# Attention, top-1 experts and a gated product on one core: when expert results leave, where two preparations stand, and which engine makes 24 low halves

## The chip, the cores and the metric

One core of a Trainium2 chip runs the whole program. The metric is the device time of one execution in microseconds (us); of the kernel before there are three runs, 886.69 to 887.77 us, median 887.34. A profiled execution is a run of its own, with its own time and span.

The engines that the text names: PE (TensorE, matrix products), ACT (ScalarE), DVE (VectorE), POOL (GpSimd) and SP (SyncE, which here only issues transfers). Each works its own list of instructions in order and waits on semaphores for the others.

## The reference

Three parts follow one another on 2304 tokens of width 512:

- attention: 4 batches x 8 heads, 576 positions of width 64, causal with a window of 128 and a slope per head; `scores = q k^T / 8 - slope * distance`, softmax over the window, times v. The heads of a token side by side are its 512 numbers x.
- top-1 experts: `e = argmax(x @ w_gate)` over 8 experts, `out = gate * sigmoid(x @ w_output_gate)[e] * (relu(x @ w1[e]) @ w2[e])`, hidden width 1024; gate is the softmax value of e.
- gated product: `g = x @ w_gate`, `out = (g * sigmoid(g) * (x @ w_val)) @ w_out`, hidden width 1536.

All is float32. The inputs are q, k and v, the experts' weights and the gated product's weights.

## The kernel before

A float32 operand is held as two halves, a high part that ACT makes by a copy into the type fp32r and a low part, the rest, that DVE or POOL makes by a subtraction. Each product is three passes (high x high, high x low, low x high), so a high and a low half of every weight and every activation have to be there in time.

**Attention and routing** (to about 160 us) go block by block over 128 tokens. For each group of blocks the routing counts the tokens of each expert and gives each token a row: DVE's `ohb` (L597, the one-hot choice), `gs` (L599, counts), `expf` (L601), `base` (L603), then PE counts those ahead, then DVE's `rk` (L616), `rankf` (L620), `sli` (L622). By `sli` the weighted tokens are scattered into the DRAM buffer `xs`, sorted by expert. At the end `expert_tables` sorts the experts by their counts, so that the experts p = 0 to 7 run from the fullest to the emptiest, with caps of 384, 384, 352, 336, 304, 272, 256 and 256 rows.

**Experts.** For p = 0 to 7 there are two products. The first makes `oh` in 8 steps m of 12 matmuls (L1089); ACT makes `hh` = relu(oh) (L1097) and DVE `hl`, the low half (L1100). The second makes the four results `oy` in 8 steps kk of 12 matmuls (L1114) from `hh` and `hl`; in its first four steps PE transposes the next expert's tokens (`tx`, L1016), which ACT and DVE split. A result leaves by `store_y`: ACT copies `oy` from PSUM to a buffer `y` (L1051) and issues its transfer to the DRAM buffer `ys` (L1053). The pool `sp` has two buffers under the tag "sc", which y shares with `sg` and `av` of the last part. At the end of an expert `store_y(2)` lets two results go, and the other two go one by one behind the next expert's steps m = 0 and m = 1; behind the last expert all four go at its end.

**Gated product** (from 414.95 us in the profile). Six units of 384 tokens, each of 12 steps (`wide_step`): `gate` and `val` (12 matmuls each, L1198); ACT's sigmoid `sg` (L1209), DVE's `sg` times gate (L1210) and `av` (L1211), ACT's `hh` (L1212), DVE's `hl` (L1213). Three steps later PE adds the step's share of the result `oo` (L1156). Tokens come by `load_unit` from `ys` (`xr<-ys`, L1026) and are split at L1034 and L1035.

**Weights** stream behind all this. SP loads them into one of LA = 7 staging buffers (`raw` of the experts, L340; `rawd` of the gated product, which are stored as 64-bit numbers, L345). A list `plan` gives each step of the experts and of the first wide unit the weights that it prepares, by `behind_step`, which calls `w_item` for each: for an expert's weight ACT's copy (L373) and a subtraction (L375) by DVE or, for each third, POOL. A half of a weight of the gated product takes `narrow`: ACT's L313 and L315, DVE's L321 and L324, and, one item later (`behind_half`), ACT's copy (L365) and the subtraction L366 on the engine that `behind_step` passes: POOL for p up to 6, DVE from the last expert on.

**Order.** From the end of attention a manual schedule holds: each engine's list is in the order in which the code is written, SP's too. Before that line a scheduler orders by dependencies. In it, before the first expert's tokens, stand `load_x(0)`, `expert_tables()`, a sigmoid of one number (L1070), 48 matmuls that keep PE busy (`keep_warm`), and `late_low`, which makes the low halves of the first expert's weights (L390) whose high halves were copied at L389.

Of the kernel before, what the change touches and what calls it, by code (L numbers as in the profile page):

```python
# [28 lines left out]
def attn_moe_glu_kernel(ctx, tc, q, k, v, w_gate, w_ogate, w1, w2, w2_gate, w2_val, w2_out, out, caps=CAPS):  # L29
    nc = tc.nc  # L30
# [63 lines left out]
    with ExitStack():  # L94
# [231 lines left out]
            )  # L326
            return lo.bitcast(F32)

        loaded = []
        sorted_known = [False]  # L330

        def w_load():
            while wjobs and len(loaded) < LA:
                name, kk, c, src = wjobs[-1]
                if name[1] > 0 and not sorted_known[0]:
                    return
                wjobs.pop()
                if c is None:
                    t = stg.tile([128, 512], F32, tag="stg", name="raw")
                    r = nc.sync.dma_start(out=t, in_=src())  # L340
                    if not sorted_known[0]:
                        tc.add_manual_dep(r.ins, pace[0].ins.name, DATA, reason="after the loads of the first rows")
                else:
                    t = stg.tile([128, 256, 2], I32, tag="stg", name="rawd")
                    nc.sync.dma_start(out=t.rearrange("p f b -> p (f b)"), in_=src())  # L345
                loaded.append((name, kk, c, t))

        w_late = []

        halves, n_rows = [], [0]  # L350

        def slot_of(name, kk, c):
            if kk % 2 == 0 and not c:
# [439 lines left out]


        wB[0] = wctx.enter_context(tc.tile_pool(name="wB", reuse_waits="tile", bufs=NBS))
        ht_p = wctx.enter_context(tc.tile_pool(name="ht", reuse_waits="tile", bufs=1))
        xe_p = wctx.enter_context(tc.tile_pool(name="xe", reuse_waits="tile", bufs=1))
        xr_p = wctx.enter_context(tc.tile_pool(name="xr", reuse_waits="tile", bufs=1))
        s_p = wctx.enter_context(tc.tile_pool(name="sp", reuse_waits="tile", bufs=2))
        tb_p = wctx.enter_context(tc.tile_pool(name="tb", reuse_waits="tile", bufs=1))  # L800
        ps_m = wctx.enter_context(tc.tile_pool(name="ps_m", reuse_waits="tile", bufs=8, space=PSUM))
# [5 lines left out]
        def tb(name, shape, dt=F32):  # L807
            return tb_p.tile([128] + shape, dt, tag=name, name=name)
# [3 lines left out]
        def scratch():  # L812
# [5 lines left out]
        TT, TS, STT, RED = (  # L818
            nc.vector.tensor_tensor, nc.vector.tensor_scalar, nc.vector.scalar_tensor_tensor, nc.vector.tensor_reduce)

        def expert_tables():

            cnt_ps = ps_m.tile([128, E], F32, tag="m", name="cnt_ps")
            for i in range(NGR):
                nc.tensor.matmul(out=cnt_ps, lhsT=ones, rhs=gs[:, i, :], start=(i == 0), stop=(i == NGR - 1))
            nc.vector.tensor_copy(cnt[:, 0, :], cnt_ps)
            key, srt = tb("key", [E]), tb("srt", [E])
            STT(out=key, in0=cnt[:, 0, :], scalar=float(E), in1=ktab, op0=ALU.mult, op1=ALU.add)
            nc.vector.max(out=srt, in_=key)
            ki, ci = tb("ki", [E], I32), tb("ci", [E], I32)  # L830
            nc.vector.tensor_copy(ki, srt)
            TS(out=reg[:, 0, :], in0=ki, scalar1=E - 1, scalar2=E - 1, op0=ALU.bitwise_and, op1=ALU.bitwise_xor)
            for p in range(1, E):
                e_reg[p] = nc.sync.value_load(reg[0:1, 0, p:p + 1], min_val=0, max_val=E - 1)
            TS(out=ci, in0=ki, scalar1=(1 << 15) - 1, scalar2=3, op0=ALU.bitwise_and, op1=ALU.logical_shift_right)
            held, end, off, ep = (tb(nm, [1, E]) for nm in ("held", "end", "off", "ep"))
            nc.vector.tensor_copy(ep[:, 0, :], reg[:, 0, :])
            nc.vector.tensor_copy(held[:, 0, :], ci)
            TT(out=held, in0=held, in1=capt, op=ALU.min)
            nc.vector.tensor_copy(end[:, :, 0:1], held[:, :, 0:1])  # L840
            for p in range(1, E):
                TT(out=end[:, :, p:p + 1], in0=end[:, :, p - 1:p], in1=held[:, :, p:p + 1], op=ALU.add)
            nc.vector.tensor_copy(total, end[:, :, E - 1:E])
            TT(out=off, in0=end, in1=held, op=ALU.subtract)
            nc.vector.tensor_copy(reg[:, 1, :], off[:, 0, :])

            own, pick = (t[:, 0:E, :] for t in scratch())
            TT(out=own, in0=iota8.unsqueeze(2).to_broadcast([128, E, E]), in1=ep.to_broadcast([128, E, E]),
               op=ALU.is_equal)
            for src, dst in ((off, offe), (capt, cape)):  # L850
                TT(out=pick, in0=own, in1=src.to_broadcast([128, E, E]), op=ALU.mult)
                RED(out=dst.rearrange("p a e -> p e a"), in_=pick, axis=AX, op=ALU.add)
# [123 lines left out]
            nc.vector.tensor_copy(er[:, 1, :], first[0:1, :, 0])  # L976
            nc.scalar.dma_start(out=ov_er[:, :, :], in_=er)

        xr, xe = {}, {}


        def raw_tile():
# [21 lines left out]
        def emit_xT(p, kks=range(KD)):  # L1004
            if p >= E:
                return
            n = caps[p]
            cb = -(-n // 128)
            r = xr[p]
            if p not in xe:  # L1010
                xe[p] = [grid(t, KD, n) for t in pair_tile(xe_p, "x", KD * cap)]
            xh, xl = xe[p]
            for kk in kks:
                t = ps_m.tile([128, CP], F32, tag="m", name="tx")
                for c in range(cb):
                    nc.tensor.transpose(t[:, c * 128:c * 128 + 128], r[:, c, kk * 128:kk * 128 + 128], ident)  # L1016
                nc.scalar.activation(out=xh[:, kk, :], in_=t[:, 0:n], func=AF.Copy)
                TT(out=xl[:, kk, :], in0=t[:, 0:n], in1=xh[:, kk, :], op=ALU.subtract)
# [38 lines left out]
        def behind_step():  # L1057
            st = step_no[0]
            step_no[0] += 1
            p = st // STEPS  # L1060
            for w in plan[st]:
                assert loaded[0][0:3] == w[0:3]
                w_item(nc.gpsimd if p < E - 1 else nc.vector)
            if p < E:
                next(tokens, None)

        with tc.manual_schedule(engines=ALL_ORDERED):
            load_x(0)
            expert_tables()
            nc.scalar.activation(out=tb("sig", [1]), in_=ident[:, 0:1], func=AF.Sigmoid)  # L1070
            sorted_known[0] = True
            keep_warm(ps_m, "m", 48)
            late_low(3)
            emit_xT(0)
            load_x(1)
# [4 lines left out]
            for p in range(E):  # L1080
# [3 lines left out]
                for m in range(KF):  # L1084
                    o = ps_m.tile([128, cap], F32, tag="m", name="oh")
                    i = 0
                    for a, b in PASSES:
                        for kk in range(KD):
                            nc.tensor.matmul(  # L1089
                                out=o[:, 0:n],  # L1090
                                lhsT=wt["w1", p, m // 4, kk][:, a, (m % 4) * 128:(m % 4) * 128 + 128],
                                rhs=(xh, xl)[b][:, kk, :],
                                start=(i == 0),
                                stop=(i == 3 * KD - 1),
                            )
                            i += 1
                    nc.scalar.activation(out=hh[:, m, :], in_=o[:, 0:n], func=AF.Relu)  # L1097
                    if p == 0 and m > 0:
                        off_reg[m] = nc.scalar.value_load(reg[0:1, 1, m:m + 1], min_val=0, max_val=NT)
                    STT(out=hl[:, m, :], in0=o[:, 0:n], scalar=0.0, in1=hh[:, m, :], op0=ALU.max, op1=ALU.subtract)  # L1100
                    if m % 4 == 3:
                        freed[0] += 2
                    store_y(1)
                    behind_step()
                    if p == E - 1 and m == 4:
                        load_unit(0)
                if p == E - 1:
                    wide_x = [[grid(t, KD, WU) for t in pair_tile(xe_p, "x", KD * cap)]]
                    x2[0] = wide_x[0]
                o = [ps_m.tile([128, cap], F32, tag="m", name="oy") for _ in range(KD)]  # L1110
                for kk in range(KF):
                    for d in range(KD):
# [17 lines left out]
                            load_x(p + 2)  # L1130
                    behind_step()
                y_left.extend((p, d, o[d][:, 0:n], n) for d in range(KD))
                store_y(2 if p < E - 1 else KD)
            load_unit(1)
            for _ in tokens:
                pass

# [77 lines left out]
        with tc.manual_schedule(engines=ALL_ORDERED):  # L1215
            for u in range(NW):
                for m in range(KF2):
                    s = u * KF2 + m
                    wide_step(u, m)
                    if u == 0:  # L1220
                        behind_step()
                        if not loaded:
                            behind_half(nc.vector)
                    if 7 <= m < 7 + KD and u + 1 < NW:
                        if m == 7:
                            x2[u + 1] = wide_x[(u + 1) % 2]
                        split_part(u + 1, m - 7)
# [134 lines left out]
```

## Time and profile before

| | |
|---|---|
| median of 3 runs | 887.34 us (886.69 to 887.77) |
| profiled execution, its own time | 891.87 us |
| its span | 890.2 us |
| mean granted clock | 0.978 of 2.4 GHz |
| PE busy | 845.7 us (95%) |
| DVE busy | 463.9 us (52%) |
| ACT busy | 396.1 us (44%) |
| POOL busy | 193.9 us (22%) |
| chain that ended last | PE 60%, DVE 13%, ACT 11%, transfers 7% |

The span is the profiled execution from its first to its last instruction; 1.7 us of its own time lie around it. In the rows further down, a time at the start of a row is in us from the span's start, the next number is how long the instruction took, and what stands in brackets is how long the engine was idle before and what ended that. "x4" joins four instructions of the same kind. ACTq and SPq are issues of transfers by ACT and SP. PEclk is the granted clock of PE as a share of 2.4 GHz.

### The profile page before, as it was taken

How to read it: one execution, taken by the hardware profiler on the slowest of the kernel's cores; microseconds unless marked ns; L12 is line 12 of the kernel's file. 1: busy time of each engine (PE TensorE's matmuls, PEld its weight loads, DVE VectorE, ACT ScalarE, POOL GpSimd, SP SyncE). 2: the span in 40 equal slices, each digit the busy share in tenths (PEclk: the TensorE clock that was granted, in tenths of full speed). 3: DMA queues.
4: the chain of work that ended last, by engine and by line, in shares of the span. 5: the costliest groups of instructions: out<-in, count | busy, mean ns of one | idle time of the engine just before them, and what ended most of it. 6: DMA issues, size and time to landing. Idle time of an engine off the chain costs nothing.

```text
span 890.2 us, 15339 instructions
## 1 busy us (share of the span) xinstructions
PE 845.7 (95%) x5463; PEld 776.5 (87%) x5463; DVE 463.9 (52%) x1268; ACT 396.1 (44%) x1063; POOL 193.9 (22%) x293
## 2 busy tenths in 40 slices
PE   7999989799999998899897999999999999999995
PEld 4777766699999998898897999999999999999994
DVE  6678886685575576567688523322322322232231
ACT  6898982163355576566666421121211212122110
POOL 3668875031122343330000010010001001001001
PEclk9999999899999999989998999999999999999998
DMA  9999522547547767665443020010002002000001
GB/s 230 261 282 243 140 73 84 178 131 218 176 143 223 249 202 237 212 218 171 146 141 121 10 71 1 1 61 11 1 1 71 1 1 72 1 1 36 1 0 38
DMA packets 103139, 99.23 MB, mean 111 GB/s; under 512 B 62098, under 2 KB 69266, under 8 KB 103058
## 3 DMA queue, kind: packets, MB, share of 16 engines
q1 hardware_dynamic: 91168, 77.13, 29.7%
q10 hardware_dynamic: 9010, 11.59, 3.7%
q0 software_dynamic: 2880, 9.48, 2.8%
q8 instruction: 44, 0.72, 0.3%
q14 instruction: 37, 0.30, 0.1%
HBM read 77.15 MB, written 21.03 MB: 110 GB/s over the span
## 4 chain that ended last, share of the span: by engine, by line
PE 60%; DVE 13%; ACT 11%; DMA 7%; issue 4%; POOL 2%; ACTq 1%; another core or an unknown queue 0%; POOLq 0%; DVEq 0%; SPq 0%
PE oo L1156 16%; PE val L1198 16%; PE gate L1198 15%; DMA ys<-y 4%; PE oy L1114 4%; ACT w L373 4%; PE oh L1089 3%; DVE rawd L321 2%; ACT p L464 2%; PE s L422 2%; DVE rawd L324 1%; DVE w L366 1%; PE o L513 1%; DVE w L375 1%; DMA rawd<-in_moe_w_gate_dram 1%
## 5 line engine op out<-in xcount | busy, mean ns | idle before, releaser
L1210 DVE TENSOR_TENSOR sg<-gate,sg 128x384 f32<-128x384 f32 x72 | 40.0, 556 | 172.5 <-ACT sg L1209 172.5
L1114 PE MATMUL oy<-hh,w 128*128 128x384 f32 (+5 forms) x512 | 124.0, 320 | 4.4 <-DVE hl L1100 4.4
L1156 PE MATMUL oo<-w,hh 128*128 128x512 f32 x360 | 122.1, 394 | 0.0
L1174 POOL DMA_INDIRECT out_dram<-xr,oid x18 | 17.3, 962 | 468.6 <-ACT xr L1172 408.3
L1209 ACT ACTIVATE sg<-gate 128x384 f32<-128x384 f32 x72 | 35.3, 490 | 163.5 <-PE gate L1198 163.5
L1212 ACT ACTIVATE hh<-av 128x384 fp32r<-128x384 f32 x72 | 37.7, 524 | 156.2 <-DVE av L1211 156.2
L1114 PEld LDWEIGHTS oy<-hh,w 128*128 128x128 f32 x512 | 90.2, 195 | 5.2 <-DVE hl L1100 5.1
L1089 PE MATMUL oh<-xh,w 128*128 128x384 f32 (+5 forms) x512 | 87.7, 311 | 0.0
L375 DVE TENSOR_TENSOR w<-raw,w 128x512 fp32r<-128x512 f32 x75 | 66.4, 892 | 39.2 <-ACT w L373 38.2
L1114 PE MATMUL oy<-hl,w 128*128 128x384 f32 (+5 forms) x256 | 80.3, 314 | 0.0
L1156 PEld LDWEIGHTS oo<-w,hh 128*128 128x128 f32 x360 | 68.2, 190 | 12.9
L1089 PEld LDWEIGHTS oh<-xh,w 128*128 128x128 f32 x512 | 78.8, 191 | 0.1
L375 POOL TENSOR_TENSOR w<-raw,w 128x512 fp32r<-128x512 f32 x37 | 49.3, 1333 | 110.5 <-ACT w L373 98.1
L1211 DVE TENSOR_TENSOR av<-val,sg 128x384 f32<-128x384 f32 x72 | 40.1, 557 | 62.1 <-PE val L1198 61.0
L1156 PE MATMUL oo<-w,hl 128*128 128x512 f32 x180 | 71.5, 397 | 0.0
L373 ACT ACTIVATE w<-raw 128x512 fp32r<-128x512 f32 x112 | 67.2, 623 | 4.5 <-ACT y L1051 3.8
L1213 DVE TENSOR_TENSOR hl<-av,hh 128x384 fp32r<-128x384 f32 x72 | 40.3, 559 | 46.6 <-ACT hh L1212 46.6
L464 ACT ACTIVATE p<-p,mn 128x128 f32<-128x128 f32 x144 | 55.8, 392 | 5.2 <-DVE mn L453 5.1
L165 POOL TENSOR_SCALAR_AFFINE_SELECT ptm<-pt 128x512 f32<-128x512 f32 x70 | 44.6, 665 | 29.3 <-ACT pt L489 28.9
L1198 PE MATMUL val<-xh,w 128*128 128x384 f32 x192 | 43.5, 347 | 7.3 <-ACT w L365 4.9
L1114 PEld LDWEIGHTS oy<-hl,w 128*128 128x128 f32 x256 | 50.0, 195 | 0.0
L1089 PE MATMUL oh<-xl,w 128*128 128x384 f32 (+5 forms) x256 | 48.4, 311 | 0.0
(258 smaller groups left out, 1775.8 us busy)
## 6 DMA issues: line engine op xcount, KB each, us to landing
raw<-in_moe_w_dram SPq DMA_DIRECT2D x128, 256.0 KB, 3.2
xs<-zrow ACTq DMA_DIRECT2D x8, 774.0 KB, 5.7
rawd<-in_moe_w_gate_dram SPq DMA_DIRECT2D x24, 256.0 KB, 5.6
rawd<-in_moe_w_val_dram SPq DMA_DIRECT2D x24, 256.0 KB, 2.6
rawd<-in_moe_w_out_dram SPq DMA_DIRECT2D x24, 256.0 KB, 3.0
xr<-xs SPq DMA_DIRECT2D x6, 774.0 KB, 4.3
xr<-ys SPq DMA_DIRECT2D x6, 768.0 KB
qr<-in_q_dram SPq DMA_DIRECT2D x16, 256.0 KB
```

The costliest lines, as they stand in the source:

```text
L165: nc.gpsimd.affine_select(out=o, in_=i, pattern=pat, compare_op=op, fill=fill, base=base, channel_multiplier=cm)
L373: nc.scalar.activation(out=s[:, 0, :], in_=t, func=AF.Copy)
L375: (nc.gpsimd if n_rows[0] % 3 == 0 else nc.vector).tensor_tensor(out=s[:, 1, :], in0=t, in1=s[:, 0, :], op=ALU.subtract)
L464: nc.scalar.activation(out=pr[:, c, :], in_=pr[:, c, :], func=AF.Exp, bias=mn[:, c:c + 1], scale=-1.0, accum_out=sums[j][:, 4 * hf + c, 0:1],)
L1089: nc.tensor.matmul(out=o[:, 0:n], lhsT=wt["w1", p, m // 4, kk][:, a, (m % 4) * 128:(m % 4) * 128 + 128], rhs=(xh, xl)[b][:, kk, :], start= ...
L1114: nc.tensor.matmul(out=o[d][:, 0:n], lhsT=wt["w2", p, 0, kk][:, a, d * 128:d * 128 + 128], rhs=(hh, hl)[b][:, kk, :], start=(kk == 0 and i ...
L1156: nc.tensor.matmul(out=o_w[u][c], lhsT=ring[b][:, r, c * 128:c * 128 + 128], rhs=wt["o", -1, 0, kk][:, a, :], start=(kk == 0 and i == 0), ...
L1198: nc.tensor.matmul(out=o, lhsT=wt[nm, -1, m // 4, kk][:, a, (m % 4) * 128:(m % 4) * 128 + 128], rhs=(xh, xl)[b][:, kk, :], start=(n == 0), ...
L1210: TT(out=sg, in0=gv[0], in1=sg, op=ALU.mult)
L1211: TT(out=av, in0=gv[1], in1=sg, op=ALU.mult)
L1212: nc.scalar.activation(out=ah, in_=av, func=AF.Copy)
L1213: nc.vector.tensor_tensor(out=al, in0=av, in1=ah, op=ALU.subtract)
```

## The change

- Results 3 and 4 of an expert go behind the next expert's steps m = 4 and 5. Those of the last expert go behind wide steps 0 and 1 of the first unit.
- The four PSUM tiles for the transposes are taken before the four of `oy`.
- `load_x(0)`, `expert_tables`, the sigmoid of one number and `keep_warm` leave the manual schedule. The sigmoid is to issue after the last Exp of the routing, the warm-up after the last matmul of the counts.
- `behind_step` gives L366 to POOL in the last expert too, and for the first item of each wide step of the first unit.
- `w_load` counts halves that are waiting for their L365 and L366 among the seven.
- `load_unit(0)` goes from m = 4 to m = 6 of the last expert, `load_unit(1)` from behind the last expert to wide step 1. Three pools are opened in another order.

```diff
-            while wjobs and len(loaded) < LA:
+            while wjobs and len(loaded) + len(halves) < LA:
...
-        ht_p = wctx.enter_context(tc.tile_pool(name="ht", reuse_waits="tile", bufs=1))
-        xe_p = wctx.enter_context(tc.tile_pool(name="xe", reuse_waits="tile", bufs=1))
-        xr_p = wctx.enter_context(tc.tile_pool(name="xr", reuse_waits="tile", bufs=1))
+        xr_p = wctx.enter_context(tc.tile_pool(name="xr", reuse_waits="tile", bufs=1))
+        xe_p = wctx.enter_context(tc.tile_pool(name="xe", reuse_waits="tile", bufs=1))
+        ht_p = wctx.enter_context(tc.tile_pool(name="ht", reuse_waits="tile", bufs=1))
...
-                nc.tensor.matmul(out=cnt_ps, lhsT=ones, rhs=gs[:, i, :], start=(i == 0), stop=(i == NGR - 1))
+                last_cnt[0] = nc.tensor.matmul(
+                    out=cnt_ps, lhsT=ones, rhs=gs[:, i, :], start=(i == 0), stop=(i == NGR - 1)).ins
...
-                t = ps_m.tile([128, CP], F32, tag="m", name="tx")
+                t = tx_ps.pop(0) if tx_ps else ps_m.tile([128, CP], F32, tag="m", name="tx")
...
-            for w in plan[st]:
+            for i, w in enumerate(plan[st]):
                 assert loaded[0][0:3] == w[0:3]
-                w_item(nc.gpsimd if p < E - 1 else nc.vector)
+                w_item(nc.gpsimd if p < E or i == 0 else nc.vector)
...
+        load_x(0)
+        expert_tables()
+        with tc.issue_after(last_exp[0]):
+            nc.scalar.activation(out=tb("sig", [1]), in_=ident[:, 0:1], func=AF.Sigmoid)
+        sorted_known[0] = True
+        with tc.issue_after(last_cnt[0]):
+            keep_warm(ps_m, "m", 48)
         with tc.manual_schedule(engines=ALL_ORDERED):
-            load_x(0)
-            expert_tables()
-            nc.scalar.activation(out=tb("sig", [1]), in_=ident[:, 0:1], func=AF.Sigmoid)
-            sorted_known[0] = True
-            keep_warm(ps_m, "m", 48)
...
-                    store_y(1)
+                    if m in (4, 5):
+                        store_y(1)
                     behind_step()
-                    if p == E - 1 and m == 4:
+                    if p == E - 1 and m == 6:
                         load_unit(0)
...
+                if p + 1 < E:
+                    tx_ps.extend(ps_m.tile([128, CP], F32, tag="m", name="tx") for _ in range(KD))
...
-                store_y(2 if p < E - 1 else KD)
-            load_unit(1)
+                store_y(2)
...
                     if u == 0:
+                        if m < 2:
+                            store_y(1)
                         behind_step()
                         if not loaded:
                             behind_half(nc.vector)
+                        if m == 1:
+                            load_unit(1)
```

On ACT, at the start of expert 5 (128x272 is its size, 128x304 that of expert 4, whose results y are), before, stand the second y of expert 4 (the first row), then its third and fourth around the first hh and the weights' copies:

```order
L1051 ACTIVATE y<-oy 128x304
L1053 ISA
L1053 DMA ys<-y 128x304
L1097 ACTIVATE hh<-oh 128x272
L1051 ACTIVATE y<-oy 128x304
L1053 ISA
L1053 DMA ys<-y 128x304
L365 ACTIVATE wx<-rawd 128x256
L373 ACTIVATE w<-raw 128x512
L1097 ACTIVATE hh<-oh 128x272
```

In the changed kernel the same place on ACT reads so, from the second y of expert 4 on:

```order
L1052 ACTIVATE y<-oy 128x304
L1054 ISA
L1054 DMA ys<-y 128x304
L1100 ACTIVATE hh<-oh 128x272
L363 ACTIVATE wx<-rawd 128x256
L371 ACTIVATE w<-raw 128x512
L1100 ACTIVATE hh<-oh 128x272
L371 ACTIVATE w<-raw 128x512
```

and the third and fourth y stand four steps later on ACT, behind the fifth and sixth hh of expert 5:

```order
L1100 ACTIVATE hh<-oh 128x272
L1052 ACTIVATE y<-oy 128x304
L1054 ISA
L1054 DMA ys<-y 128x304
L371 ACTIVATE w<-raw 128x512
L1100 ACTIVATE hh<-oh 128x272
L1052 ACTIVATE y<-oy 128x304
L1054 ISA
L1054 DMA ys<-y 128x304
```

What moved are two copies of results with their issues, past four hh and the weights between them.

On DVE, in the routing of the last group of blocks, before, no low half stands among the routing's steps:

```order
L597 TENSOR_TENSOR ohb<-iota8m,mn 128x16
L599 TENSOR_REDUCE gs<-ohb 128x8
L601 TENSOR_TENSOR expf<-mn,iota8m 128x2
L603 TENSOR_TENSOR base<-expf,rows_e 128x2
L616 TENSOR_TENSOR rk<-g_2496,ohb 128x16
L620 TENSOR_REDUCE rankf<-rk 128x2
L622 TENSOR_TENSOR sli<-base,rankf 128x2
```

and in the changed kernel DVE has there:

```order
L595 TENSOR_TENSOR ohb<-iota8m,mn 128x16
L388 TENSOR_TENSOR w<-raw,w 128x512
L597 TENSOR_REDUCE gs<-ohb 128x8
L599 TENSOR_TENSOR expf<-mn,iota8m 128x2
L388 TENSOR_TENSOR w<-raw,w 128x512
L601 TENSOR_TENSOR base<-expf,rows_e 128x2
L614 TENSOR_TENSOR rk<-g_2496,ohb 128x16
L388 TENSOR_TENSOR w<-raw,w 128x512
L618 TENSOR_REDUCE rankf<-rk 128x2
L620 TENSOR_TENSOR sli<-base,rankf 128x2
```

Three low halves of the first expert's weights (L388, before L390) have moved up among the routing's steps, the third between rk and rankf.

On DVE, in a wide step of the first unit, before, behind the step's own hl:

```order
L1213 TENSOR_TENSOR hl<-av,hh 128x384
L321 SCALAR_TENSOR_TENSOR rawd<-rawd 128x256
L324 SCALAR_TENSOR_TENSOR rawd<-rawd 128x256
L366 TENSOR_TENSOR w<-rawd,w 128x256
L321 SCALAR_TENSOR_TENSOR rawd<-rawd 128x256
L324 SCALAR_TENSOR_TENSOR rawd<-rawd 128x256
L366 TENSOR_TENSOR w<-rawd,w 128x256
```

and in the changed kernel:

```order
L1218 TENSOR_TENSOR hl<-av,hh 128x384
L321 SCALAR_TENSOR_TENSOR rawd<-rawd 128x256
L324 SCALAR_TENSOR_TENSOR rawd<-rawd 128x256
L321 SCALAR_TENSOR_TENSOR rawd<-rawd 128x256
L324 SCALAR_TENSOR_TENSOR rawd<-rawd 128x256
L364 TENSOR_TENSOR w<-rawd,w 128x256
```

The subtraction behind the first L324 is now in POOL's list; those behind the others stay.

## Rows read from the trace of the kernel before

**Rows 1.** Waits of PE, 165 to 480 us: line, releaser, us, times, longest.

```profile
PE oy L1114 <- DVE hl L1100: 4.4, 3, 1.9
...
PE oid_ps L910 <- DVE tbl L904: 0.6, 1, 0.6
```

**Rows 2.** Stretches: length, busy PE, PEld, DVE, ACT, POOL; PEclk, DMA.

```profile
332.29:344.29 12.00, 12.00 (x99) 12.00 (x98) 4.93 (x8) 6.68 (x17) 3.03 (x4) 1.00 0.75 235
344.29:361.99 17.70, 14.91 (x107) 14.47 (x105) 14.14 (x26) 13.12 (x34) 8.02 (x8) 0.90 0.75 240
361.99:373.50 11.51, 11.51 (x98) 11.51 (x97) 4.24 (x7) 4.77 (x12) 2.79 (x3) 1.00 0.69 223
373.50:391.75 18.25, 15.49 (x106) 14.99 (x105) 14.01 (x27) 14.07 (x36) 8.05 (x9) 0.81 0.66 210
```

**Rows 3.** Chain of waits in the second product of expert 0: start, us, what.

```profile
188.58 0.33 PE tx L1016 x3
```

**Rows 4.** Waits of ACT, 165 to 480 us.

```profile
ACT y L1051 <- DMA ys<-y: 25.6, 9, 4.6
```

**Rows 5.** Timeline of ACT in the first products of experts 5 and 6.

```profile
336.78 0.40 ACT L1097 ACTIVATE hh<-oh 128x272 fp32r<-128x272 f32 x1 [0.41 <-ACT y L1051]
340.55 0.42 ACT L1051 ACTIVATE y<-oy 128x304 f32<-128x304 f32 x1 [3.38 <-DMA ys<-y]
...
367.34 0.38 ACT L1097 ACTIVATE hh<-oh 128x256 fp32r<-128x256 f32 x1 [0.42 <-ACT y L1051]
371.25 0.40 ACT L1051 ACTIVATE y<-oy 128x272 f32<-128x272 f32 x1 [3.53 <-DMA ys<-y]
```

**Rows 6.** Timeline of PE, wide step 8 of the first unit.

```profile
473.31 0.69 PE L1198 MATMUL val<-xh,w 128*128 128x384 f32 x1 [4.27 <-ACT w L365]
```

**Rows 7.** Timelines of ACT and DVE in wide steps 4 and 5.

```profile
445.01 0.47 ACT L1209 ACTIVATE sg<-gate 128x384 f32<-128x384 f32 x1
450.87 0.47 ACT L1209 ACTIVATE sg<-gate 128x384 f32<-128x384 f32 x1
...
444.54 0.42 DVE L366 TENSOR_TENSOR w<-rawd,w 128x256 fp32r<-128x256 f32 x1
444.87 0.42 DVE L321 SCALAR_TENSOR_TENSOR rawd<-rawd 128x256 int32<-128x256 int32 x1
```

**Rows 8.** Timeline of SP in the last expert.

```profile
393.17 14.47 SPq L345 DMA_DIRECT2D rawd<-in_moe_w_val_dram  x8
```

**Rows 9.** Timeline of ACT from the last expert's end to the first wide sigmoid.

```profile
412.31 0.53 ACT L1034 ACTIVATE xh<-xr 128x384 fp32r<-128x384 f32 x1 [4.62 <-DMA xr<-ys]
...
424.31 0.39 ACT L1051 ACTIVATE y<-oy 128x256 f32<-128x256 f32 x1 [2.38 <-DMA ys<-y]
...
426.62 1.28 ACT L1209 ACT_TABLE_LOAD   x1 [0.45 <-DMA ys<-y]
427.92 0.49 ACT L1209 ACTIVATE sg<-gate 128x384 f32<-128x384 f32 x1
```

**Rows 10.** Timelines of DVE and POOL, 255 to 275 us: subtractions alone and side by side.

```profile
261.82 0.69 DVE L375 TENSOR_TENSOR w<-raw,w 128x512 fp32r<-128x512 f32 x1
...
270.16 1.48 DVE L375 TENSOR_TENSOR w<-raw,w 128x512 fp32r<-128x512 f32 x1 [0.22 <-ACT w L373]
...
263.92 0.75 POOL L366 TENSOR_TENSOR wx<-rawd,wx 128x256 fp32r<-128x256 f32 x1 [2.45 <-ACT wx L365]
...
269.74 1.36 POOL L375 TENSOR_TENSOR w<-raw,w 128x512 fp32r<-128x512 f32 x1 [0.35 <-ACT w L373]
```

**Rows 11.** Chain of waits in the first 30 us.

```profile
10.48 1.28 ACT L464
...
11.77 3.20 ACT p L464 x16
```

**Rows 12.** Timeline of DVE between attention and the experts.

```profile
153.25 0.17 DVE L616 TENSOR_TENSOR rk<-g,ohb 128x16 f32<-128x16 f32 x1 [3.56 <-remote]
...
160.91 1.88 DVE L390 TENSOR_TENSOR w<-raw,w 128x512 fp32r<-128x512 f32 x3
```

More of the change, by code (lines that the diff above doesn't have):

```diff
@@ L327, in narrow @@
             return lo.bitcast(F32)
-        loaded = []
+        loaded, halves, n_rows = [], [], [0]
         sorted_known = [False]
         def w_load():
-            while wjobs and len(loaded) < LA:
+            while wjobs and len(loaded) + len(halves) < LA:
                 name, kk, c, src = wjobs[-1]
@@ L348, in attn_moe_glu_kernel @@
         w_late = []
-        halves, n_rows = [], [0]
         def slot_of(name, kk, c):
@@ L819, in attn_moe_glu_kernel @@
             nc.vector.tensor_tensor, nc.vector.tensor_scalar, nc.vector.scalar_tensor_tensor, nc.vector.tensor_reduce)
+        last_cnt = [None]
         def expert_tables():
@@ L977, in overflow_tables @@
             nc.scalar.dma_start(out=ov_er[:, :, :], in_=er)
-        xr, xe = {}, {}
+        xr, xe, tx_ps = {}, {}, []
         def raw_tile():
```

## The prediction

> **What bounds the kernel now.** I read the page first: TensorE (PE) is busy 95% of the span, and from about 480 us to the end nothing holds it. So only its pauses before that, and what moves them, can change the time. The list of what PE waited for between 165 and 480 us then shows a surprise: for the experts' second product it has three waits of together 4.4 us [rows 1], yet the table by stages has two such stages that are too long by more [rows 2]. An expert has a first product (L1089, 96 matmuls) and a second one (L1114, 96 matmuls, with four transposes of the next expert's tokens between). Expert 5 takes 12.00 us for the first and 17.70 for the second; expert 6 takes 11.51 and 18.25. The second product of each needs only the first's time plus the transposes: 0.33 us for three blocks [rows 3], so about 0.22 for two, four times 0.9. What is over, 17.70 - 12.00 - 0.9 = 4.8 us and 18.25 - 11.51 - 0.9 = 5.8 us, is waiting, spread thin between matmuls, at a granted clock of 0.90 and 0.81 of 2.4 GHz where the stages beside it have 1.00. What PE waits for there is DVE's hl (L1100) [rows 1]; hl needs ScalarE's (ACT's) hh (L1097).
>
> Next I ask what makes ACT late: its list of waits is led by the result copy y (L1051), which waits 25.6 us for ys<-y, the store of an earlier y [rows 4]. Two buffers serve y, so the third copy waits until the first store has landed. ACT works its list in order, and in the stretch around experts 5 and 6 the reader sees it stand 3.38 and 3.53 us at the third y, with the next hh of the same expert queued behind it [rows 5].
>
> **The change part by part.**
>
> Stores of results 3 and 4. They move from the next expert's first two steps to its fifth and sixth, four steps of 1.5 us later (12.00 us / 8 steps, [rows 2]), when the first store has landed: its waits go. What is late next is ACT's own speed. From the first hh of expert 5 to that of expert 6 ACT takes 367.34 - 336.78 = 30.56 us [rows 5], of which 3.38 is the wait: 27.2. PE without the excess needs 12.00 + 12.00 + 0.9 = 24.9. ACT so falls 2.3 us behind in that expert, less than the 5 us of waiting that it now skips, and I cost the excess at nothing left: -4.8 and -5.8. Smaller ends: the wait of 0.6 on the table at L904 [rows 1], as DVE and ACT are freer there, and -0.1 in expert 4. Together -11.3; bounds 0 (ACT is the limit anyway, a rival below) and -11.3, near the latter since the stall rows are of this wait itself.
>
> From the last expert to the wide product. PE's last long pause is 4.27 us at 473.31, for a weight half that ACT converts (L365) [rows 6]; up to there the wide steps run at ACT's and DVE's pace, 450.87 - 445.01 = 5.86 us [rows 7], so this chain sets the end, and I follow it from the start of the last expert.
> - The load of the first wide tokens (xr<-ys) is issued later by one weight transfer. SP spends 14.47 us on eight such issues [rows 8], 1.8 each, as each waits for a buffer. Between 0 and +1.8: the middle, +0.9. ACT waits for that load in [rows 9] (4.62 us), so it counts.
> - From there to the first sigmoid (L1209): before, the third y waits until 424.31, then a fourth, then 1.28 us of table load, and the sigmoid starts at 427.92 [rows 9]. After, two y are left and the table is loaded; the sigmoid takes the buffer of the first y and waits for the same store, to 424.31: -3.6.
> - Results 3 and 4 of the last expert come in wide steps 0 and 1 instead: two copies of 0.39 [rows 9] and their issues, which I take as long: +1.2 of ACT.
> - POOL instead of DVE makes 24 low halves: 12 in the last expert, one in each wide step of the first unit. DVE needs 0.42 for one and starts the next thing 0.33 later [rows 7], POOL 0.75 [rows 10]. Beside POOL, a DVE subtraction of the same kind (L375) took 1.48 us where it takes 0.69 alone; it started inside POOL's 1.36 us and ended 0.54 after it, which is nearly the whole of a lone one [rows 10]: it was held until POOL was done. After the change, DVE has the next half's L321 and L324 right at the time of POOL's subtraction. Per op between -0.33 (never held, only relieved) and 0.75 - 0.33 = +0.42 (held for all of it). I take +0.37 for 6 of the 12 in the last expert, +2.2, the others lying in DVE's idle time, and +0.3 in 8 wide steps before the pause at 473.31, +2.4.
>
> By the Trainium skill ("SBUF — State Buffer", SBUF: two separate sides) a DVE op with two SBUF inputs and a GpSimd op that reads SBUF lock each other out for a whole instruction, the first to start wins; [rows 10] agree with it. It speaks against this part of the change, and its strictest reading is a rival below.
>
> Chain to the wide product: 0.9 - 3.6 + 1.2 + 2.2 + 2.4 = +3.1.
>
> Start. The sigmoid table is no longer loaded among the first blocks; with it goes the reload before the first Exp, which stands on the chain of waits with 1.28 us [rows 11]. -1.0, between -1.28 and 0, as input loads or PE's work beside it may end last instead.
>
> The Trainium skill ("ScalarE: Activation LUTs", What ACT_TABLE_LOAD costs) states 1.28 us for the load and 1.38 us for a drain, 2.66 us for a switch. The trace shows the load and the Exp 0.01 us behind its end [rows 11]; by the Trainium skill the term would be -2.7 and the sum 1.7 us lower, by the row -1.28 at most.
>
> Between attention and the experts. DVE now makes three low halves among the routing steps. Two fall where it idles 3.56 us before rk [rows 12]; the third stands between rk and rankf, on the path to the scatter of the tokens: 1.88 / 3 = 0.63 [rows 12], +0.65 with its issue, between 0 and +1.3 (two of them). In return the 1.88 us at 160.91 go [rows 12], where no chain stands on DVE. Pools in another order, the warm-up outside the written order, the table loads of SP and the staging count: nothing, since PE's order is unchanged and [rows 1] show no wait on such loads in this stretch.
>
> Sum: -11.3 + 3.1 - 1.0 + 0.65 = -8.55. The profiled execution took 891.87 us, so a like one would take 883.3; the median before is 887.34, 4.5 lower, and I put the sum on that: **878.8 us**.
>
> **The rivals.**
> - *POOL does not hold L321 and L324 up.* They are bit operations on integers, and no row shows one held. For it: none; against: [rows 10] with another op. Then DVE is only relieved: the lock's +4.6 becomes about -1.2 (0.15 in each of 8 steps, as ACT paces the rest). 878.8 - 5.8 = 873.0.
> - *It holds them in full, every time.* 20 ops (12 + 8) at 0.42 are 8.4 instead of 4.6: 882.6. Against it stands that DVE has idle time (busy for 14.01 of 18.25 us even in the stage of expert 6 that waits for it, [rows 2]), so some are held where it would idle. (It is the lock of the Trainium skill, named above, taken strictly.)
> - *The excess of experts 5 and 6 stays (slower).* ACT needs 27.2 us where PE needs 24.9, and y 3 and 4 now stand in steps 5 and 6, close to the second product. Decides: if the hl of step 5 of expert 6 is later than 1.1 us after the second product's start (nine matmuls of 0.12, 11.51 / 96), PE waits as before. Then -0.7 is left of -11.3: 878.8 + 10.6 = 889.4. Against: [rows 5] put the wait itself in front of hh.
> - *The change doesn't free the copies.* sg and av share y's two buffers, and stores may land as late. About 887.
>
> **How the numbers follow.** Chances: forecast 0.52, no hold 0.22, full hold 0.16, excess stays 0.07, no effect 0.03. The forecast's own range is 875 to 882 (the ends of the issue, start and rank terms). The low end: no hold, with table -1.28, no cost of rank and issue: 873.0 - 0.3 - 0.65 - 0.9 = 871.1. The high: full hold with +1.0, +0.65 and +0.9: 885.1. Range 871.5 to 885. This kernel's runs tell about 0.2%, 1.8 us, from no change; faster by more holds the first three cases, 0.90; same holds the last and a little of the fourth, 0.04; slower the rest of that, 0.06.
>
> **What would show it.** ACT's wait of y on ys<-y falls from 25.6 to under 5; the second products of experts 5 and 6 take about 12.9 and 12.4 at clock 1.00; the first wide sigmoid starts some 12 us earlier (-11.65 + 0.9 - 3.6 + 2.2), with no table load before it; the wide step is 6.2 instead of 5.86; L321 and L324 take over 0.42 us beside POOL. The pause before the Exp is 1.28 shorter. It is wrong if the two second products stay near 18 us, or if wide steps get shorter.

## The result, and the profile after

The changed kernel takes 879.4 us (median of 4 runs, 876.57 to 880.19) against 887.56 for the one before: a ratio of 0.9903, with a 95% interval of 0.9878 to 0.9927. The forecast was 878.8 us. The profiled execution after took 880.19 us, with a span of 878.5.

The waits of PE, 165 to 480 us, in the changed kernel (line and releaser, us in total, times, longest; the columns of [rows 1]):

```profile
PE val L1203 <- ACT w L363: 8.3, 3, 4.8
PE gate L1203 <- ACT xh L1035: 4.7, 4, 1.4
PE tx L1017 <- DMA xr<-xs: 2.8, 1, 2.8
PE val L1203 <- DVE sg L1215: 0.2, 1, 0.2
```

The rows of oy on hl and of the table at L904 [rows 1] are gone; what is left of waiting is for the first expert's tokens (tx), at the first wide unit's start (gate) and in its wide steps (val). The same four stretches of experts 5 and 6 as in [rows 2], read off the windows:

```profile
327.97:340.00 12.03, 12.03 (x99) 12.03 (x98) 7.58 (x15) 8.63 (x22) 4.34 (x5) 1.00 0.94 311
340.00:352.90 12.90, 12.90 (x106) 12.90 (x106) 9.99 (x19) 9.74 (x25) 5.86 (x6) 1.00 0.75 227
352.90:364.20 11.30, 11.30 (x99) 11.30 (x98) 7.05 (x13) 7.21 (x19) 4.42 (x5) 1.00 0.81 270
364.20:376.10 11.90, 11.90 (x106) 11.90 (x105) 9.50 (x19) 9.22 (x25) 4.72 (x5) 1.00 0.82 251
```

The second products went from 17.70 to 12.90 us and from 18.25 to 11.90; PE is busy in all of them, and the granted clock is 1.00 where it was 0.90 and 0.81. The list of ACT's waits, whose first row was y on ys<-y with 25.6 us [rows 4], has no such row any more. Three waits that were shorter have grown (the last stood before a table load, 0.5 us):

```profile
ACT hh L1100 <- PE oh L1092: 27.9, 30, 2.2
ACT xh L1035 <- DMA xr<-ys: 6.7, 1, 6.7
...
ACT sg L1214 <- DMA ys<-y: 2.3, 1, 2.3
```

hh waits for PE, 27.9 us where it was 22.4 before. The tokens' load is waited for 2.1 us longer than in [rows 9], more than the 0 to 1.8 of the prediction. The first sigmoid waits for the store of result 1, as forecast. In the first wide unit, ACT, DVE and POOL in one step (timelines of the three engines; [rows 7] show the step of before):

```profile
431.84 0.51 ACT L1214 ACTIVATE sg<-gate 128x384 f32<-128x384 f32 x1
...
436.76 0.44 ACT L363 ACTIVATE w<-rawd 128x256 fp32r<-128x256 f32 x1 [0.53 <-DVE rawd L324]
...
438.07 0.48 ACT L1214 ACTIVATE sg<-gate 128x384 f32<-128x384 f32 x1
...
435.33 0.42 DVE L321 SCALAR_TENSOR_TENSOR rawd<-rawd 128x256 int32<-128x256 int32 x1 [0.15 <-ACT rawd L315]
435.79 0.93 DVE L324 SCALAR_TENSOR_TENSOR rawd<-rawd 128x256 int32<-128x256 int32 x1
436.65 0.41 DVE L321 SCALAR_TENSOR_TENSOR rawd<-rawd 128x256 int32<-128x256 int32 x1
437.10 0.43 DVE L324 SCALAR_TENSOR_TENSOR rawd<-rawd 128x256 int32<-128x256 int32 x1
...
435.69 0.75 POOL L364 TENSOR_TENSOR w<-rawd,w 128x256 fp32r<-128x256 f32 x1 [5.48 <-DMA rawd<-in_moe_w_gate_dram]
```

The step takes 438.07 - 431.84 = 6.23 us where it took 5.86. The reader sees why: POOL's subtraction starts at 435.69, L324 at 435.79, and that L324 takes 0.93 us, to just behind POOL's end (436.44), where the next one takes 0.43. ACT then waits 0.53 for it. Over the whole kernel (durations in ns, shortest / median / longest) the longest L324 is 996 now, 433 before:

```profile
L324 DVE SCALAR_TENSOR_TENSOR rawd<-rawd x72: 425/427/996, 257.2 to 489.5; 128x256 int32<-128x256 int32 x72
```

The two profiled spans differ by 11.7 us, the timed medians by 8.2. The rest of 3.5 is probably a loss of the one profiled execution of before. There DVE waited 3.56 us before rk [rows 12]; later PE stood 5.40 us before the first transposes, and its granted clock was then 0.50 of 2.4 GHz (1.2 GHz) from 166 to 170 us. From the first transposes to expert 0's second product it took 186.34 - 165.56 = 20.78 us. In the changed kernel PE stood 2.8 us there, the clock was 1.00, and the same piece took 183.45 - 164.71 = 18.74 us. In the changed kernel, b1, b3 and n4 the wait at rk is at most 0.2 us. With one profile of the kernel before this stays an argument.

The changed kernel's routing reads:

```profile
150.36 0.17 DVE L595 TENSOR_TENSOR ohb<-iota8m,mn 128x16 bf16<-128x16 f32 x1
150.57 0.69 DVE L388 TENSOR_TENSOR w<-raw,w 128x512 fp32r<-128x512 f32 x1
...
151.33 0.68 DVE L388 TENSOR_TENSOR w<-raw,w 128x512 fp32r<-128x512 f32 x1
...
152.00 0.17 DVE L614 TENSOR_TENSOR rk<-g,ohb 128x16 f32<-128x16 f32 x1
152.09 0.68 DVE L388 TENSOR_TENSOR w<-raw,w 128x512 fp32r<-128x512 f32 x1
152.69 0.16 DVE L618 TENSOR_REDUCE rankf<-rk 128x2 f32<-128x16 f32 x1
```

### The profile page after: what moved, and what is told of

It reads as the page before. It is cut to its first block, busy times and chain, and to the rows that moved or that the text cites. A ratio compares the mean times of both kernels' runs of the same rounds, so it can differ in the third digit from the quotient of the medians.

```text
span 878.5 us, 15367 instructions
## 1 busy us (share of the span) xinstructions
PE 838.6 (95%) x5463; PEld 767.6 (87%) x5463; DVE 467.3 (53%) x1244; ACT 393.9 (45%) x1061; POOL 212.2 (24%) x317
## 4 chain that ended last, share of the span: by engine, by line
PE 46%; DVE 2%; ACT 1%; issue 1%; POOL 0%; POOLq 0%; DVEq 0%; ACTq 0%
PE oo L1161 16%; PE val L1203 15%; PE gate L1203 15%; DVE rawd L324 1%; DVE rawd L321 1%; ACT rawd L313 0%; ACT rawd L315 0%; DVE av L1216 0%; DVE sg L1215 0%; DVE w L364 0%; ACT w L363 0%; POOL out_dram L1179 0%; POOLq L1258 0%; DVE xr L1175 0%; ACT xr L1174 0%
## 5 line engine op out<-in xcount | busy, mean ns | idle before, releaser
L1215 DVE TENSOR_TENSOR sg<-gate,sg 128x384 f32<-128x384 f32 x72 | 40.0, 556 | 168.0 <-ACT sg L1214 168.0
L1120 PE MATMUL oy<-hh,w 128*128 128x384 f32 (+5 forms) x512 | 118.3, 311 | 0.0
L1120 PEld LDWEIGHTS oy<-hh,w 128*128 128x128 f32 x512 | 86.5, 188 | 0.0
L1120 PE MATMUL oy<-hl,w 128*128 128x384 f32 (+5 forms) x256 | 78.5, 307 | 0.0
L373 DVE TENSOR_TENSOR w<-raw,w 128x512 fp32r<-128x512 f32 x75 | 63.7, 856 | 24.9 <-ACT w L371 23.1
L1216 DVE TENSOR_TENSOR av<-val,sg 128x384 f32<-128x384 f32 x72 | 40.1, 557 | 62.3 <-PE val L1203 60.5
L1120 PEld LDWEIGHTS oy<-hl,w 128*128 128x128 f32 x256 | 48.2, 188 | 0.0
```

What stands on the lines that cost most here:

```text
L373: (nc.gpsimd if n_rows[0] % 3 == 0 else nc.vector).tensor_tensor(out=s[:, 1, :], in0=t, in1=s[:, 0, :], op=ALU.subtract)
L1120: nc.tensor.matmul(out=o[d][:, 0:n], lhsT=wt["w2", p, 0, kk][:, a, d * 128:d * 128 + 128], rhs=(hh, hl)[b][:, kk, :], start=(kk == 0 and i ...
L1215: TT(out=sg, in0=gv[0], in1=sg, op=ALU.mult)
L1216: TT(out=av, in0=gv[1], in1=sg, op=ALU.mult)
```

## The experiments

The kernel before ran beside them at medians of 888.47 (n1, n2, n3, b1), 887.91 (n4, n5, v1, b3) and 887.85 us (v3, v1 again).

**b1, the stores alone.** On the kernel before:

```diff
-                    store_y(1)
+                    if m in (4, 5):
+                        store_y(1)
...
-                store_y(2 if p < E - 1 else KD)
-            load_unit(1)
+                store_y(2)
```

and with it the last expert's results 3 and 4 in wide steps 0 and 1, the tiles for tx, the counting of halves and the units' loads, as in the change.

> The kernel before, with the stores moved as in the change and what they need (PSUM tiles for the transposes taken earlier, units loaded later, halves counted among the staging buffers); start, order and POOL as before. Theory: 887.5 - 11.3 for the excess, - 2.3 for the sigmoid that no longer waits for two more copies (its table load stays), + 1.2 for two copies in the wide steps, + 1 to 2 for the later load: 875 to 877. Rival (stores do nothing alone): 886 to 888.

Measured: 876.79 us (875.09 to 877.22), ratio 0.9864 (0.9845 to 0.9883), inside the theory's range. Windows of experts 5 and 6 (second products) and of the last expert's first:

```profile
339.26:352.19 12.93, 12.93 (x106) 12.93 (x105) 10.03 (x19) 9.79 (x25) 5.89 (x6) 1.00 0.76 235
...
363.70:376.08 12.38, 12.38 (x106) 12.38 (x105) 9.97 (x19) 9.73 (x26) 5.06 (x6) 1.00 0.81 252
376.08:387.60 11.52, 11.52 (x98) 11.52 (x97) 9.19 (x22) 8.96 (x28) 2.00 (x2) 1.00 0.68 206
```

Moving the stores, with what goes along, takes the whole excess away. That kernel's median is 2.6 us below the full change's, so something in the rest of the change costs.

**n3, the stores as before.** On the changed kernel:

```diff
-                    if m in (4, 5):
-                        store_y(1)
+                    store_y(1)
...
-                store_y(2)
+                store_y(2 if p < E - 1 else KD)
...
-                        if m < 2:
-                            store_y(1)
```

> The changed kernel, with results 3 and 4 leaving in the next expert's first and second step and all four at the last expert's end, as before. Theory (the stores' place makes the excess of experts 5 and 6): second products of experts 5 and 6 at 17 to 18 us again, first sigmoid late again: 888 to 892. Rival (the excess went by the other parts: warm-up, pools in another order, PSUM tiles taken earlier): 879 to 881.

Measured: 889.92 us (12 runs), ratio 1.0019 (1.0005 to 1.0033): without the stores' move, the rest makes the kernel slower. Its waits of ACT and its stretch of expert 5's second product:

```profile
ACT y L1052 <- DMA ys<-y: 24.6, 9, 3.7
```

```profile
339.33:356.54 17.21, 14.64 (x107) 14.19 (x105) 13.66 (x26) 12.61 (x33) 7.75 (x8) 0.90 0.72 240
```

Expert 6 takes 13.01 and 16.30 us for its two products (from 356.54, to 369.55 and to 385.85). The wait and the excess come back together. With b1 this shows the cause from both sides.

**n1 and n2, POOL's low halves.** On the changed kernel, one line:

```diff
-                w_item(nc.gpsimd if p < E or i == 0 else nc.vector)
+                w_item(nc.gpsimd if p < E - 1 else nc.vector)
```

and in n2 `p < E` instead of `p < E - 1`.

> The changed kernel (879.4 us), with all low halves of the last expert and of the wide steps on DVE again. Theory (POOL's subtraction holds DVE's L324 up): L324 never takes longer than 0.43 us, the wide step goes from 6.2 back to 5.86 us, the last expert's items lose their waits, about 4 us faster: 874.5 to 876.5. Rival (POOL only relieves DVE, the longer wide step has another cause such as later weight loads): the same 879.4 or up to 1.5 us slower, wide step still 6.2.

> The changed kernel, with POOL making the 12 low halves of the last expert and DVE those of the wide steps. Theory by the prediction's two terms (2.2 in the last expert, 2.4 in the wide steps): halfway, about 877. If the whole cost is in the wide steps: as with none on POOL, about 875. If it is in the last expert: about 879.

Measured: n1 874.13 us (871.69 to 876.52), ratio 0.9841 (0.9817 to 0.9864); n2 875.25 (874.29 to 876.03), ratio 0.9849 (0.9831 to 0.9868). In n1 ACT's wide step and the durations of L324 are

```profile
426.43 0.47 ACT L1214 ACTIVATE sg<-gate 128x384 f32<-128x384 f32 x1
...
432.28 0.47 ACT L1214 ACTIVATE sg<-gate 128x384 f32<-128x384 f32 x1
```

```profile
L324 DVE SCALAR_TENSOR_TENSOR rawd<-rawd x72: 425/426/431, 254.4 to 481.1; 128x256 int32<-128x256 int32 x72
```

so 5.85 us again and none over 0.431. Each price is read from the start of the last expert to PE's long pause in wide step 8 (in [rows 6] at 473.31, 81.56 us behind that start): the changed kernel at 461.95 - 376.12 = 85.83, n2 at 457.48 - 374.64 = 82.84, n1 at 454.72 - 373.38 = 81.34. So POOL costs 3.0 us in the wide steps and 1.5 in the last expert, by one profile of each kernel. The 1.5 is the weaker of the two: the intervals of n1 and n2 overlap, and n2's 875.25 us is what was expected if the last expert cost nothing. PE's row of that pause in n2, as an example of the three:

```profile
457.48 0.69 PE L1203 MATMUL val<-xh,w 128*128 128x384 f32 x1 [4.27 <-ACT w L363]
```

**n5, POOL at the third item.** On the changed kernel: `w_item(nc.gpsimd if p < E - 1 or p == E and i == 2 else nc.vector)`.

> The changed kernel, with the last expert's low halves on DVE and, in each wide step of the first unit, POOL making the low half that comes up at the third item instead of the first. Behind it DVE has L1215 and L1216, which read one operand from PSUM, and not another L321. Theory (only a DVE op with both inputs in SBUF is held): DVE is relieved by 0.33 and not held, the wide step is about 5.5 us, 2 to 3 us faster than with all on DVE (874.1): 871 to 872.5. Rival (POOL holds any DVE op that comes beside it): wide step 6.2 again, 876 to 878.

Measured: 876.53 us (873.45 to 876.96), ratio 0.986 (0.9841 to 0.9878): a miss. POOL starts before L324 here too, so it holds that one and not L1215 (timelines of DVE and POOL):

```profile
429.83 0.93 DVE L324 SCALAR_TENSOR_TENSOR rawd<-rawd 128x256 int32<-128x256 int32 x1
430.69 0.55 DVE L1215 TENSOR_TENSOR sg<-gate,sg 128x384 f32<-128x384 f32 x1
...
429.73 0.75 POOL L364 TENSOR_TENSOR w<-rawd,w 128x256 fp32r<-128x256 f32 x1 [5.27 <-ACT w L363]
```

The wide step is 435.55 - 429.51 = 6.04 us, not 5.5. The expectation had the place wrong, not what is held; v3 puts it right.

**n4, the start as before.** On the changed kernel, `load_x(0)` to `keep_warm` are back inside the manual schedule.

> The changed kernel, with the first load of tokens, the expert tables, the sigmoid of one number and the warm-up in the written order again, as before. Theory by the prediction (table load at the start -1.0, a low half between rk and rankf +0.65): 0.35 us slower than the changed kernel, 879.8. If the table load counts in full and the low half not: 880.7. If the whole part costs (the low half on the routing's path, nothing won at the start): 878.5. The Exp's table load is back at about 10 us, and rk and rankf stand side by side.

Measured: 880.08 us (879.13 to 880.49), ratio 0.9911 (0.9898 to 0.9925), against 0.9903 for the whole change: no difference that these runs tell. The edit also brings a table load back in front of the first wide sigmoid (1.28 us at 410.56), and from the last expert's start to PE's long pause n4 takes 461.79 - 375.06 = 86.73 us against 85.83. So n4 prices the start together with that load. The reload before the first Exp is back:

```profile
11.88 1.28 ACT L462 ACT_TABLE_LOAD   x1
13.17 0.40 ACT L462 ACTIVATE p<-p,mn 128x128 f32<-128x128 f32 x1
```

From the first copy qk to the first p it is 13.17 - 7.50 = 5.67 us here and 11.58 - 7.34 = 4.24 in the changed kernel, 1.43 less. The routing is the other side of it:

```profile
150.91 0.17 DVE L595 TENSOR_TENSOR ohb<-iota8m,mn 128x16 bf16<-128x16 f32 x1
...
151.51 0.17 DVE L614 TENSOR_TENSOR rk<-g,ohb 128x16 f32<-128x16 f32 x1
151.72 0.17 DVE L618 TENSOR_REDUCE rankf<-rk 128x2 f32<-128x16 f32 x1
```

From ohb to rankf it is 0.81 us here and 152.69 - 150.36 = 2.33 in the changed kernel, 1.52 more: two low halves hold rk back by 1.04 and the third holds rankf back by 0.48. PE's first transposes come 11.93 us behind rankf here and 12.02 there, so these 1.5 us do reach the experts, and they are as much as the start gives. From the first copy to rk the three later kernels with the start as before (n4, b3, b1) have 144.0 to 144.5 us; of eight profiles with the changed start, five have 144.2 to 145.1 (the changed kernel, n3, n5, v1 and its repeat) and three 142.7 to 143.1 (n1, n2, v3). What sets those three apart stays open.

**b3, the pools' order alone.** On the kernel before, `xr` and `ht` opened in the changed order.

> The kernel before, with only the three pools opened in the changed order. What is open: in all kernels with the changed order a matmul of the last expert's first product comes each 0.113 us (10.88 us for 96), in those with the order before each 0.120 (11.52). Theory (where the operands lie makes it): 10.9 us here. Rival (another part of the change makes it): 11.5 us. The time stays within 887 to 889 either way, as the excess of experts 5 and 6 is there.

Measured, one run: 884.27 us, and the last expert's first product takes neither time:

```profile
383.56:394.87 11.31, 11.31 (x99) 11.31 (x97) 5.60 (x12) 6.49 (x20) 2.22 (x2) 1.00 0.60 183
```

11.31 us, 0.118 for a matmul. n3, with the pools' order but the stores as before, has 0.118 as well; the changed kernel 0.113. b1, with the stores' move and the pools' order of before, has 0.120. So the pools' order alone gives a third of it, the stores' move alone nothing, and the rest came where both were there; what sets it stays open. The time missed the expected 887 to 889 us: expert 5's second product took 353.35 - 338.96 = 14.39 us here instead of 17.70, while expert 6's kept 17.64. Whether the pools' order or this one execution did that is open; n3, with the same order, has 17.21 and 16.30.

**v1, the split behind the weight items.** On n1:

```diff
-                        else:
-                            split_part(0, kk)
...
                 store_y(2)
+                for kk in range(KD):
+                    split_part(0, kk)
```

> The changed kernel with all low halves on DVE (874.1 us), and the split of the first unit's tokens (L1035, L1036) behind the last expert's weight items and the copies of results 1 and 2 instead of among them. In the kernel without this ACT stands 7.1 us waiting for the tokens' load, with the six items and the two copies behind that wait, and the first sigmoid then waits 2.7 us more for the store of result 1. Theory (that order sets the chain to the wide product): six items of 1.05 us fit into the wait, the first sigmoid starts 6 to 7 us earlier, 867 to 869. Rival (the items' own loads are not there yet, as SP loads in order): 873 to 875.

Measured: 869.77 us (869.0 to 870.9), ratio 0.9799 (0.9786 to 0.9813), and beside v3 869.0, ratio 0.9789 (0.9766 to 0.9813). ACT at the last expert's end:

```profile
398.29 0.36 ACT L1052 ACTIVATE y<-oy 128x256 f32<-128x256 f32 x1
...
399.92 1.77 ACT L1035 ACTIVATE xh<-xr 128x384 fp32r<-128x384 f32 x4 [0.42 <-ACT y L1052]
403.67 0.49 ACT L1214 ACTIVATE sg<-gate 128x384 f32<-128x384 f32 x1 [1.98 <-PE gate L1203]
```

The six items fit into the wait for the tokens, the sigmoid comes 403.67 - 376.38 = 27.3 us behind the last expert's start (n1: 407.80 - 373.38 = 34.4), and it waits for PE, not for a store. The repeat was expected so:

> The kernel v1 a second time, beside v3 on one chip: 869 to 871.

**v3, POOL behind L324.** On v1, POOL makes one low half in a wide step, at the third item, and waits for that item's L324:

```diff
+                on_pool = p == E and i == 2
-                w_item(nc.gpsimd if p < E - 1 else nc.vector)
+                w_item(nc.gpsimd if p < E - 1 or on_pool else nc.vector, on_pool)
...
+                if after is not None:
+                    tc.add_manual_dep(r.ins, after.name, DATA, reason="beside DVE's reads of PSUM")
```

> The kernel v1 (869.8 us: all low halves on DVE, tokens split behind the weight items), with POOL making one low half in each wide step of the first unit, at the third item, and told to start only when that item's L324 is done. So POOL's 0.75 us lie beside DVE's L1215 and L1216, which read PSUM. Theory (only DVE ops with two SBUF inputs are held, and DVE paces the wide step): no L324 over 0.43, wide step 5.5 us instead of 5.86, PE's pause of 3.6 us in wide step 8 falls to about 1: 866.5 to 868. Rival (POOL holds L1215 or L1216 as well): wide step 5.9 to 6.2, 870 to 872. Second rival (ACT, not DVE, paces the step): wide step 5.86 with nothing held, 869 to 870.5.

Measured: 866.42 us (863.53 to 866.84), ratio 0.9749 (0.9725 to 0.9774), the fastest of all. DVE, POOL and ACT in one wide step (L326 is L324 here, L1220 and L1221 are L1215 and L1216):

```profile
423.52 0.43 DVE L326 SCALAR_TENSOR_TENSOR rawd<-rawd 128x256 int32<-128x256 int32 x1
423.87 0.55 DVE L1220 TENSOR_TENSOR sg<-gate,sg 128x384 f32<-128x384 f32 x1
424.52 0.56 DVE L1221 TENSOR_TENSOR av<-val,sg 128x384 f32<-128x384 f32 x1
...
424.21 0.75 POOL L366 TENSOR_TENSOR w<-rawd,w 128x256 fp32r<-128x256 f32 x1 [4.78 <-DVE rawd L326]
...
423.19 0.48 ACT L1219 ACTIVATE sg<-gate 128x384 f32<-128x384 f32 x1
428.73 0.47 ACT L1219 ACTIVATE sg<-gate 128x384 f32<-128x384 f32 x1
```

POOL's 0.75 us lie beside the two operations that read PSUM (L1221 starts inside them), these keep their 0.55 and 0.56, and the step is 5.54 us: DVE is relieved by 0.33 and held by nothing. PE's pause in wide step 8 is 1.23 us:

```profile
449.83 0.45 PE L1208 MATMUL val<-xh,w 128*128 128x384 f32 x1 [1.23 <-ACT w L365]
```

## Why the prediction was right

The time, 878.8 forecast and 879.4 measured, and the mechanism of the large term were right; b1 and n3 show that this term has the cause that the prediction gave. That the total is only 0.6 us off is partly luck: the stores' part and expert 1 gave 1.1 us more than forecast, the chain cost 1.2 more, and start and rank came to about nothing where -0.35 stood.

- **The stores, -11.3.** Expert 5's second product: -4.8 forecast, 17.70 to 12.90 measured. Expert 6: -5.8 forecast, 29.76 to 23.20 for its two products, -6.6. The 0.7 more is a part that no step had: a matmul of 256 columns comes each 0.113 to 0.118 us instead of 0.120. The wait at L904: -0.6 forecast; expert 1 went from 36.13 to 35.11, but it takes 235.81 - 200.71 = 35.10 in b3 too, where the stores are as before, so that part is not shown to be theirs. ACT's 27.2 us in an expert against PE's 24.9 did not come through as a new wait, and the slower rival (the excess stays) falls; so does the one in which the copies aren't freed, as ACT has no wait of y on ys<-y left.
- **The chain to the wide product, +3.1.** It measured 85.83 - 81.56 = +4.3. To the first sigmoid: 36.17 us behind the last expert's start before, 411.41 - 376.12 = 35.29 after, -0.9, where 0.9 - 3.6 + 2.2 = -0.5 stood in the forecast. Two errors cancel in it. The tokens' split starts 398.83 - 376.12 = 22.71 us behind that start against 20.56, +2.15 for the load where +0.9 stood: SP issues it 1.03 later, and it takes 5.62 us to land instead of 4.50. From there to the sigmoid it is 12.58 against 15.61, -3.0 where -1.4 stood. In the profiles the first wide sigmoid came 16.5 us earlier instead of 12; 15.6 of it is there at the last expert's start already (391.75 against 376.12), where the forecast had 11.65. In the wide steps +1.2 for two copies and +2.4 for POOL were forecast, 3.6; it is 4.3 + 0.9 = 5.2. The terms that were too small are in steps 0 and 1: from the first to the third sigmoid 425.67 - 411.41 = 14.26 us against 439.14 - 427.92 = 11.22, so +3.0. n1, with the same copies and no POOL there, has 420.58 - 407.80 = 12.78, +1.6 for the copies with what waits behind them.
- **POOL holds DVE up, +4.6.** n1 and n2 measure 3.0 + 1.5 = 4.5, split 2.4 and 2.2 in the forecast. L321, which the prediction also named, is not held in the changed kernel (0.457 us at most); L324 alone carries it. The rival without a hold falls by L324's 0.93 us and by n1, which is faster, not slower. The rival that is held in full (+8.4) falls by these 4.5. The rule that the prediction quoted from the Trainium skill ("SBUF — State Buffer", SBUF: two separate sides) agrees with these traces in which operations are held: L324, with two SBUF inputs, is held; L1220 and L1221, with one from PSUM, are not (v3).
- **The start, -1.0, and the rank, +0.65.** At the start 1.43 us go locally. By the Trainium skill ("ScalarE: Activation LUTs", What ACT_TABLE_LOAD costs) it would be 2.66; the traces don't agree. The rank term was too small: from ohb to rankf it is 2.33 us against 0.81 in n4, +1.5, above the prediction's bound of 1.3. By these rows the two terms cancel, and n4 can't be told from the whole change.
- **A reading that failed.** It is behind that rank term. The prediction took the 3.56 us before rk as idle time of each execution, into which two low halves would fall. No later profile has that wait; from ohb to rk it is 0.60 us without the low halves and 1.64 with them, so the two cost 1.04 where nothing stood. The wait probably has a large part, too, in the 4.5 us that the profiled execution took above the median, which the prediction noted and did not explain.

## What to carry to other kernels

A wait on a buffer that is still being stored stands in front of everything behind it on an engine that works in order: look for it in that engine's list of waits before asking why PE waits for something further down, and move the copies to where the stores have landed. Giving work to an idle engine pays only if it doesn't hold the busy one: 24 subtractions on POOL cost 4.5 us beside DVE operations with two SBUF inputs, 3.0 of it for the 12 in the wide steps; 12 in the wide steps beside those that read PSUM won 2.6 (869.0 to 866.42). And an engine that waits for a load may as well do the work that is listed behind that wait: that order alone gave about 4 us (874.13 to 869.77).

## What the runs showed of the hardware that was not expected

- The spacing of matmuls with 256 columns in the last expert's first product, at a granted clock of 1.00, was 0.120 us in the kernel before and b1, 0.118 with the pools in another order and the stores as before (b3, n3), and 0.113 with both (the changed kernel, n1, n2, n4, n5, v1 twice and v3: 10.88 us for 96 in each profile). Its cause stays open.
- A DVE operation that comes 0.10 us after POOL's start ends 0.28 us behind POOL's end (435.79 + 0.93 = 436.72 against 436.44), less than the 0.43 that it takes alone: it takes 0.50 longer, of POOL's 0.75. In all 23 held ones of the changed kernel the end is 0.27 to 0.29 us behind POOL's, whatever the start: they began 0.04 to 0.29 us behind the start of POOL's. This fits an operation that stands until POOL is done and then has 0.28 left, so that 0.15 of its 0.43 went by before.
